# Batch 0 without expert pieces, batch 1 in units of 256, constant matmuls in waits, and expert 1's weights issued later

## The chip, the cores and the metric

The kernel runs on one core of one Trainium2 chip. The metric is the device time of one execution in microseconds (us); lower is better. TensorE (PE in the profile) does the matmuls, VectorE (DVE) and ScalarE (ACT) read their results out of PSUM, GpSimd (POOL) casts and issues the transfers that convert weights to 16 bits, and SyncE (SP) issues all other transfers. PEld is TensorE's loading of the stationary operand.

## What is computed

Attention with a sliding window of 128 and a linear bias over 8 batches of 576 positions with 8 heads of 64, and behind it a layer of 8 experts over all 4608 tokens, each token's experts weighted by a table P that comes out of 8 rounds of row and column normalisation:

```python
scores = scale * np.matmul(q, k.transpose(0, 1, 3, 2))
scores = np.where(mask, scores + bias[None], -1000000000.0)
attn = np.exp(scores - np.max(scores, axis=-1, keepdims=True))
x = (attn / attn.sum(-1, keepdims=True)) @ v      # then [4608, 512]
P = np.exp(x @ w_gate - max)
for _ in range(8):
    P /= P.sum(1, keepdims=True) + 1e-09
    P /= P.sum(0, keepdims=True) + 1e-09
    P *= N / E
for e in range(E):
    out += P[:, e:e + 1] * (np.maximum(x @ w1[e], 0.0) @ w2[e])
```

## The kernel before

**Two parts.** The first 340 us hold the attention of the 8 batches and, woven into it, experts 0 and 1, which do not need P: their results go to a scratch tensor and are weighted later. The rest of the time belongs to the normalisation and to experts 2 to 7 over 18 groups of tokens. The change is in the first part only.

**The order is written out by hand.** The kernel says in which order instructions stand; each engine takes its own in exactly that order, and waits at the first that isn't ready. Nothing overtakes. The same holds for the two queues of transfers: SyncE's (q1 in the profile) and GpSimd's (q0).

**A batch.** Its q and k come in as 1 MB each (`load_qk`, L232), v in five blocks of 128 positions (`load_v`, L334; the last has 64), the last 64 rows of q and k as a "tail" (`load_tail`, L223). `cast_qk(b, j)` (L247 for k on ScalarE, L245 for q on VectorE) converts a quarter of the heads to 16 bits. For batches 0 to 2 TensorE turns them (`turn_pe`, L311, eight 128-wide transposes for the k and q of one quarter), and ScalarE (L326) and VectorE (L324) copy the result out of PSUM. From batch 3 on DMA transposes do it. `cast_v` on GpSimd (L344) converts v.

**A step** is one block of 128 keys and one half of the heads: ten steps in a batch, written here (batch, block, half) or as step 0 to 9. `scores` (L372, L379) is four or eight matmuls, `exps` (L390) one exponential on ScalarE, `masks` (L403) one product with a table on VectorE (window and bias in one; `make_mask`, L209, makes the table on ScalarE with eight exponentials), `values` (L426) the product with v, of which a column of ones gives the denominator; VectorE takes the reciprocal (L436) and multiplies (L437). After both halves `turn_x` (L457) transposes the block and a copy (L465) puts it into xT, the experts' input. In the order of the code the next step's scores and exponential stand ahead of this step's values.

**The filler.** A unit is (expert, first block, number of blocks). Its layer 1 is 8 pieces (L102: 4 matmuls each, 128 columns for each block, then a ReLU on ScalarE, L109), its layer 2 one piece for each block (L115: 8 matmuls of 512 columns, then a copy by VectorE, L495 or L499). `Filler.take` hands out one piece; `fill(us)` hands out pieces until their planned cost (0.87 us for a layer-1 piece of 4 blocks, half of it for 2, 1.74 for a layer-2 piece) is used up. A unit can start when its blocks are in xT (`ready`) and its expert's weights are allowed (`allowed`). A step's `budget` spreads what is ready over the steps that are left.

**Weights.** `load_weights(e)` (L86, L88) issues w1 and w2 of an expert on GpSimd's queue, 1 MB each as stored. Expert 1's are issued after step 1 of batch 0, allowed from step 4 of batch 1.

**Buffers.** Four PSUM buffers ("pmm") go round among transposes, values, layer 1 and layer 2; two more hold scores. Staging buffers for v and the tails: five; SyncE issues a load once the buffer's last reader is done.

## Time and profile before

| | us |
|---|---|
| median of 3 runs | 1060.77 (1059.07 to 1062.29) |
| the profiled execution | 1060.31 |
| its span | 1058.5 |
| TensorE busy | 1031.1 (97%), 9006 matmuls |
| VectorE, ScalarE, GpSimd busy | 631.7, 434.5, 77.4 |
| TensorE busy in 0 to 10, 10 to 20, 20 to 30 | 3.44, 8.07, 6.15 |
| TensorE busy in 50 to 60, 60 to 70, 70 to 80 | 6.70, 9.40, 10.00 |
| mean granted clock of TensorE | 0.998 |

The profile comes from one execution. Its page has the span in 40 slices of 26.5 us, with the busy tenths of each engine, the granted clock of TensorE in tenths, and the busy share of the 16 DMA engines. The views of the trace give the same by stretches of chosen length; a list in order of time gives the start, the length, the engine, the line, the operation and, in brackets, how long the engine sat idle before it and what released it. A line of the waits is: who waited for whom, us in total, times, longest. A line of the chain is: start, length, what. A line of a DMA queue is: packets, MB, share of the 16 engines. [...]

### The profile page before, as it was taken

How to read it: one execution, taken by the hardware profiler on the slowest of the kernel's cores; microseconds unless marked ns; L12 is line 12 of the kernel's file. 1: busy time of each engine (PE TensorE's matmuls, PEld its weight loads, DVE VectorE, ACT ScalarE, POOL GpSimd, SP SyncE). 2: the span in 40 equal slices, each digit the busy share in tenths (PEclk: the TensorE clock that was granted, in tenths of full speed). 3: DMA queues.
4: the chain of work that ended last, by engine and by line, in shares of the span. 5: the costliest groups of instructions: out<-in, count | busy, mean ns of one | idle time of the engine just before them, and what ended most of it. 6: DMA issues, size and time to landing. Idle time of an engine off the chain costs nothing.

```text
span 1058.5 us, 21148 instructions
## 1 busy us (share of the span) xinstructions
PE 1031.1 (97%) x9006; PEld 802.9 (76%) x9006; DVE 631.7 (60%) x1171; ACT 434.5 (41%) x729; POOL 77.4 (7%) x139
## 2 busy tenths in 40 slices
PE   6789999999999999999999999999999999999998
PEld 4455444444544888888888888888888888888887
DVE  4655665655687665655655655655655655555555
ACT  6556555555233333333333333333333333333332
POOL 2112032325100000000000000000000000000000
PEclk9999999999999999999999999999999999999999
DMA  9985599879992501211211210211220220220240
GB/s 226 252 221 139 114 201 218 196 154 177 182 207 70 115 23 49 71 26 46 71 39 33 70 49 23 71 39 32 71 65 7 71 68 3 71 71 1 71 90 20
DMA packets 166110, 98.55 MB, mean 93 GB/s; under 512 B 84960, under 2 KB 157440, under 8 KB 166016
## 3 DMA queue, kind: packets, MB, share of 16 engines
q1 hardware_dynamic: 151280, 79.21, 29.4%
q0 software_dynamic: 14304, 17.84, 10.2%
q8 instruction: 70, 1.15, 0.4%
q14 instruction: 24, 0.20, 0.1%
q10 hardware_dynamic: 432, 0.16, 0.1%
HBM read 87.74 MB, written 19.02 MB: 101 GB/s over the span
## 4 chain that ended last, share of the span: by engine, by line
PE 92%; DMA 4%; SPq 2%; DVE 1%; ACT 1%; issue 0%; POOL 0%; ACTq 0%
PE psh L834 36%; PE psS_m L889 31%; PE psh L102 11%; PE psy L115 10%; DMA v<-in_v_dram 2%; DMA k<-in_k_dram 2%; PE psN L426 1%; PE psS L372 1%; DMA xT<-xsb 1%; SPq L334 1%; SPq L223 0%; SPq L288 0%; PE psy L954 0%; PE psG L473 0%; ACT hT L109 0%
## 5 line engine op out<-in xcount | busy, mean ns | idle before, releaser
L841 ACT ACTIVATE hs<-psh 128x512 f16<-128x512 f32 x432 | 258.0, 597 | 453.2 <-PE psh L834 373.7
L834 PE MATMUL psh<-aux,w1l 128*128 128x256 f16 x2880 | 372.6, 273 | 0.2 <-ACT hs L841 0.2
L834 PEld LDWEIGHTS <-w1l 128*128 128x128 f16 x2880 | 281.7, 98 | 33.3 <-issue 0.5
L889 PEld LDWEIGHTS <-hs 128*128 128x128 f16 x2568 | 251.3, 98 | 29.1
L846 DVE TENSOR_TENSOR hs<-hs 128x1024 f16<-128x1024 f16 x107 | 74.1, 693 | 274.5 <-ACT hs L841 274.3
L889 PE MATMUL psS_m<-w2l,hs 128*128 128x256 f16 x1440 | 186.6, 273 | 0.0
L102 PE MATMUL psh<-xT,w1t 128*128 128x512 f16 (+1 forms) x640 | 141.1, 359 | 4.4 <-DMA xT<-xsb 1.7
L115 PE MATMUL psy<-w2t,hT 128*128 128x512 f16 x576 | 133.8, 379 | 3.4 <-DMA w2t<-in_moe_w_dram 2.8
L818 DVE TENSOR_TENSOR aux<-xT,pbc 128x1024 f16<-128x1024 f16 x108 | 131.4, 1217 | 2.5 <-DMA pbc<-ptd 2.5
L109 ACT ACTIVATE hT<-psh 128x512 f16<-128x512 f32 (+1 forms) x160 | 87.6, 556 | 100.6 <-PE psh L102 99.3
L115 PEld LDWEIGHTS <-hT 128*128 128x128 f16 x576 | 53.7, 98 | 64.6 <-issue 4.8
L102 PEld LDWEIGHTS <-w1t 128*128 128x128 f16 x640 | 57.9, 99 | 53.6 <-issue 6.4
L390 ACT ACTIVATE pt<-psS 128x1024 f16<-128x1024 f32 (+2 forms) x80 | 67.5, 852 | 45.9 <-PE psS L372 37.0
L935 DVE TENSOR_TENSOR acc<-acc,psS_m 128x256 f32<-128x256 f32 (+1 forms) x162 | 74.3, 504 | 12.4 <-PE psS_m L889 11.1
L499 DVE CAST yo<-psy 128x512 f16<-128x512 f32 x68 | 46.9, 690 | 55.5 <-PE psy L115 54.3
L403 DVE TENSOR_TENSOR pt<-pt,mask 128x1024 f16<-128x1024 f16 (+2 forms) x80 | 50.2, 627 | 41.5 <-ACT pt L390 41.4
L889 PE MATMUL psS_m<-more,hs 128*128 128x256 f16 x576 | 74.6, 273 | 0.0
L834 PE MATMUL psh<-aux,w1t 128*128 128x256 f16 x576 | 74.6, 273 | 0.0
L849 DVE TENSOR_TENSOR hs<-hs 128x1024 f16<-128x1024 f16 x107 | 73.2, 684 | 0.0
L834 PEld LDWEIGHTS <-w1t 128*128 128x128 f16 x576 | 56.4, 98 | 6.5
L535 POOL DMA_DIRECT2D w2t<-in_moe_w_dram x2 | 1.8, 878 | 705.2 <-PE psS_m L889 669.8
L426 PEld LDWEIGHTS <-pt 128*128 128x128 f16 (+2 forms) x576 | 28.6, 101 | 26.1 <-DVE pt L403 6.8
(83 smaller groups left out, 657.2 us busy)
## 6 DMA issues: line engine op xcount, KB each, us to landing
pbc<-ptd SPq DMA_DIRECT2D x108, 128.0 KB, 4.5
y<-ysp SPq DMA_DIRECT2D x36, 256.0 KB, 4.7
ysp<-yo SPq DMA_DIRECT2D x68, 128.0 KB, 3.1
v<-in_v_dram SPq DMA_DIRECT2D x32, 256.0 KB, 3.9
out_dram<-acc SPq DMA_DIRECT2D x31, 256.0 KB, 2.4
q<-in_q_dram SPq DMA_DIRECT2D x7, 1024.0 KB, 6.4
k<-in_k_dram SPq DMA_DIRECT2D x7, 1024.0 KB, 9.8
w2t<-in_moe_w_dram POOLq DMA_DIRECT2D x4, 1024.0 KB, 14.7
```

What stands on the lines that cost most here:

```text
L102: nc.tensor.matmul(out=ps[:, 0:nt], lhsT=w1ts[e][:, dt, P * ft : P * ft + P], rhs=xT[:, b0 : b0 + nb, dt, :], start=(dt == 0), stop=(dt == ...
L109: nc.scalar.activation(out=st["hT"][:, ft, 0:nt], in_=ps[:, 0:nt], func=AF.Relu)
L115: nc.tensor.matmul(out=ps, lhsT=st["hT"][:, ft, P * ms : P * ms + P], rhs=w2ts[e][:, ft, :], start=(ft == 0), stop=(ft == NFT - 1),)
L390: nc.scalar.activation(out=pt[0:nk, :, 0 : nk + nn], in_=ps[0:nk, :, :, 0 : nk + nn].rearrange("p a y n -> p (a y) n"), func=AF.Exp, scale ...
L403: nc.vector.tensor_tensor(out=pt[0:nk, :, 0:w], in0=pt[0:nk, :, 0:w], in1=mask[0:nk, hs, 0:w], op=ALU.mult)
L818: nc.vector.tensor_tensor(out=xs(n).rearrange("p (d b t) -> p d b t", d=NDT, b=2), in0=xT[:, 2 * g : 2 * g + 2].rearrange("p b d t -> p d ...
L834: nc.tensor.matmul(out=ps[:, f, :], lhsT=W1L[e][:, dt, P * ft : P * ft + P], rhs=xs(n)[:, HB * dt : HB * dt + HB], start=(dt == 0), stop=( ...
L841: nc.scalar.activation(out=h[n][:, 2 * i : 2 * i + 2, :], in_=ps, func=AF.Relu)
L846: nc.vector.tensor_tensor(out=t[:, NFT : NFT + NF2, :], in0=a[:, 0:NF2, :], in1=a[:, NF2:NFT, :], op=ALU.add)
L849: nc.vector.tensor_tensor(out=t[:, NFT + NF2 : 2 * NFT, :].rearrange("p f n -> p (f n)").rearrange("p (f t) -> p f t", t=P), in0=a[:, :, P ...
L889: nc.tensor.matmul(out=Ms[g, bank][:, half, :], lhsT=left(n, m, f), rhs=W2L[e][RIGHT[m]][:, f, :], start=(e == 2 and f == 0 and half == 0) ...
L935: nc.vector.tensor_tensor(out=a, in0=a, in1=p2, op=op)
```

## The change

It makes these edits, all in the first part:

- Batch 0 takes no filler pieces, but for two layer-1 pieces in each of steps 6 and 7. At the end of batch 0 all layer-1 pieces of its four blocks that are left (12 of 16) stand in one stretch, then two layer-2 pieces, then batch 1's first transposes (`hold`, `budget`, the loop with `filler.take()`). Layer 2 is held back until there.
- The blocks 4 to 7 (batch 1) form two units of two blocks each for both experts, in place of one unit of four: 64 more matmuls, each half as wide.
- `spin` adds matmuls of 256 columns on a constant tile (the tile of ones, read as 16-bit numbers), whose results nobody reads: 20 at the start, 4 before and after batch 0's first scores and before its second transposes, 8 after the long layer-1 stretch, and 3 ahead of the value matmuls of each step of batch 0 and of steps 0 to 5 of batch 1: 88 in all.
- The second half of the mask table is made in two parts between the first casts; the first mask product stands behind the transposes.
- In batch 0 ScalarE copies x into xT, in place of VectorE.
- Expert 1's weights are issued after step 7 of batch 0 (on GpSimd's queue behind three more casts of v), and its units are allowed after step 8 of batch 1.
- Batch 2's casts and transposes move from steps 3 to 7 of batch 1 to steps 5 to 8. The load of batch 3's q and k stays at step 3 of batch 1, and its first cast at the end of step 8.

The order of SyncE's queue stays the same up to batch 2's last block of v.

```diff
     ident = per.tile([P, P], FP16, name="ident")
     ident32 = per.tile([P, P], FP32, name="ident32")
     ones32 = per.tile([P, P], FP32, name="ones32")
+    junk = ones32.bitcast(FP16)
     wg_sb = per.tile([P, NDT, E], FP16, name="wg_sb")
     rs_sb = per.tile([P, NBLK], FP32, name="rs_sb")
     cs_sb = per.tile([P, E], FP32, name="cs_sb")
...
             self.since = 0
             self.ready = 0
             self.allowed = {0}
+            self.hold = True
 
         def start_unit(self):
             for n, (e, b0, nb, make) in enumerate(self.todo):
...
             if not self.l1 and len(self.l2) <= 2:
                 if self.start_unit():
                     self.since = 0
-            use_l2 = bool(self.l2) and (not self.l1 or self.since >= 2)
+            use_l2 = bool(self.l2) and not self.hold and (not self.l1 or self.since >= 2)
             if use_l2:
                 self.l2.pop(0)()
                 self.since = 0
...
         mask = asb.tile([P, H, 2 * P], FP16, name="mask")
         rel = per.tile([P, HD], FP16, name="rel", tag="yo", bufs=YO)[:, 0 : 2 * P]
 
-        def make_mask(u):
-            for y in range(4 * u, 4 * u + 4):
+        def make_mask(ys):
+            for y in ys:
                 nc.scalar.activation(
                     out=mask[:, y, :], in_=rel, func=AF.Exp, scale=-float(slopes[head_of[y]])
                 )
...
         KT: dict = {}
         QKT: dict = {}
         vs: dict = {}
+
+        def spin(ps, n):
+
+            for _ in range(n):
+                nc.tensor.matmul(out=ps[:, 0 : 2 * P], lhsT=junk[:, 0:P], rhs=junk, start=True, stop=True)
+
+        spins = [0]
+
+        def spin_alone(n):
+            spins[0] += 1
+            spin(aps.tile([P, GT], FP32, name=f"psJ_{spins[0]}", tag="pmm", bufs=4), n)
 
         def load_tail(b):
             t32 = asb.tile([P, H, Dh], FP32, name=f"t32_{b}", tag="s32", bufs=5)
...
             if u == 0:
                 xsbs[b, kb] = asb.tile([P, H, Dh], FP16, name=f"xsb_{b}_{kb}", tag="xsb", bufs=3)
             psN = aps.tile([P, GT], FP32, name=f"psN_{b}_{kb}_{u}", tag="pmm", bufs=4)
+            if b == 0 or (b == 1 and 2 * kb + u < 6):
+                spin(psN, 3)
             psN = psN[:, 0 : 4 * Dh + 4].rearrange("p (h d) -> p h d", h=4)
             ops = []
             for y in range(2):
...
                         start=(j == 0),
                         stop=(j == NDT - 1),
                     )
-                nc.vector.tensor_copy(out=to, in_=ps[:, :, 0:nk])
+                if b == 0:
+                    nc.scalar.copy(out=to, in_=ps[:, :, 0:nk])
+                else:
+                    nc.vector.tensor_copy(out=to, in_=ps[:, :, 0:nk])
             else:
                 nc.sync.dma_start(out=to, in_=xsb[0:nk].rearrange("p h d -> p (h d)"), transpose=True)
 
...
             nc.vector.tensor_copy(out=yo, in_=ps)
             stores.append((e, blk, yo))
 
-        spans = [(0, 2), (2, 2)] + [(4 * g, 4) for g in range(1, NG)]
+        spans = [(2 * g, 2) for g in range(4)] + [(4 * g, 4) for g in range(2, NG)]
         order = [(0, 0), (0, 1)]
         for n in range(2, len(spans)):
             order += [(0, n), (1, n - 2)]
...
         nc.scalar.dma_start(out=rel, in_=rel_h.ap())
         nc.scalar.dma_start(out=ident, in_=ident_h.ap())
         nc.scalar.dma_start(out=ident32, in_=ident32_h.ap())
+        nc.vector.memset(ones32, 1.0)
         load_first()
-        nc.vector.memset(ones32, 1.0)
-        make_mask(0)
+        spin_alone(20)
+        make_mask(range(4))
         cast_v(0)
         load_weights(0, 0, 1)
         cast_v(1)
...
         steps = [(b, kb, u) for b in range(B) for kb in range(NKB) for u in range(2)]
         for j in range(2):
             cast_qk(0, j)
+            make_mask((4 + 2 * j, 5 + 2 * j))
+            if j:
+                spin_alone(4)
             turn_pe(0, 1, j)
             turn_pe(0, 0, j)
         cast_qk(0, 2)
         cast_qk(0, 3)
+        spin_alone(4)
         scores(*steps[0])
         exps(*steps[0])
+        spin_alone(4)
         turn_pe(0, 1, 2)
         turn_pe(0, 0, 2)
-        masks(*steps[0])
         turn_pe(0, 1, 3)
         turn_pe(0, 0, 3)
-        make_mask(1)
+        masks(*steps[0])
         for n, (b, kb, u) in enumerate(steps):
             nxt = steps[n + 1] if n + 1 < len(steps) else None
             at = 2 * kb + u
             left = ((8 if b < XPE else 10) - at) % 10 + 1
             budget = filler.backlog() / (11 if (b, at) == (XPE, 0) else left)
+            if b == 0:
+                budget = 1.0 if at in (6, 7) else 0.0
             if nxt:
                 if nxt[0] < XPE and nxt[1:] == (RI - 2, 1):
                     turn_pe(nxt[0], 0, NDT)
                 if nxt == (1, 0, 0):
+                    filler.ready = RI
+                    while filler.l1 or filler.todo[0][1] < RI:
+                        filler.take()
+                    filler.hold = False
+                    spin_alone(8)
+                    filler.fill(3.6)
                     cast_qk(1, 0)
                     cast_qk(1, 1)
                     for j in range(NDT):
...
                     scores(*nxt)
                     scores(*nxt[:2], 1)
                 exps(*nxt)
-            got = filler.fill(1.0)
+            got = filler.fill(1.0) if b else 0.0
             if nxt:
                 masks(*nxt)
             values(b, kb, u)
...
                     gates(4 * b - 4, 4 * b)
                 if n // 2 + NKB + 1 < B * NKB:
                     load_v(n // 2 + NKB + 1)
-            if b == 0 and at == 1:
+            if b == 0 and at == 7:
                 load_weights(1)
+            if (b, at) == (1, 8):
+                filler.allowed.add(1)
             if b == 1 and at == 4:
-                filler.allowed.add(1)
                 nc.sync.dma_start(out=ysp[0, 0:RI].rearrange("m p d -> p m d"), in_=first_y[0])
             if (b, at) == (0, 3):
                 load_qk(2)
...
                 homes(1)
             if (b, at) == (1, 3):
                 homes(2)
-            if b == 1 and 3 <= at <= 6:
-                cast_qk(2, at - 3)
-            if b == 1 and 4 <= at <= 7:
-                turn_pe(2, 1, at - 4)
-                turn_pe(2, 0, at - 4)
+            if b == 1 and 5 <= at <= 8:
+                for j in ((), (0, 1), (2,), (3,))[at - 5]:
+                    turn_pe(2, 1, j)
+                    turn_pe(2, 0, j)
+                for j in ((0, 1), (2,), (3,), ())[at - 5]:
+                    cast_qk(2, j)
             if 1 <= b < B - 2 and at == 3:
                 load_qk(b + 2)
             if 1 <= b < B - 2 and at >= 8:
```

## The prediction

> **What bounds the kernel now.** I read the page's slices first, then the chain of work that ended last for 35 to 75 us, then the waits up to 70 us, and last the DMA queues in stretches of 2 us.

> ```profile
> PE   6789999999999999999999999999999999999998
> PEclk9999999999999999999999999999999999999999
> DMA  9985599879992501211211210211220220220240
> ```

> TensorE is short of work only in the first three slices (79 us), and there the DMA engines are full. From 66 us to the end TensorE loses about 7 us in all. So the change can win only what the start loses, and the start is fed by DMA.

> ```profile
> 37.10 17.45 DMA k<-in_k_dram
> 54.55 0.03 ACTq L247
> ...
> 54.62 0.62 ACT c L247
> 55.23 0.49 ACT tT L320
> ...
> 57.96 1.55 PE psh L102 x8
> ...
> 66.71 0.87 PE psh L102 x8
> ...
> 72.54 1.73 PE psy L115 x8
> ```

> Batch 2's k takes 17.45 us to land. ScalarE's cast of it stands in the middle of batch 1 (L247, in program order), so ScalarE and then TensorE stop:

> ```profile
> ACT c L247 <- DMA k<-in_k_dram: 5.8, 3, 2.9
> PE psX L457 <- ACT tT L320: 2.9, 1, 2.9
> ```

> After that gap the granted clock is half, and eight 256-wide matmuls take 1.55 us where they take 0.87 at 66.71:

> ```profile
> 56.00:58.00 2.00, 2.00 (x29) 1.66 (x27) 1.29 (x4) 1.95 (x4) 0.00 (x0) 0.50 1.25 223
> ```

> Why does k take so long? Expert 1's weights are issued at 38.28 and share the engines. In 40 to 42 us SyncE's queue (q1) is alone; in 46 to 48 and in 52 to 54 it runs beside w1 and w2 on GpSimd's queue (q0):

> ```profile
> q1 hardware_dynamic: 620, 0.62, 96.8%
> ```

> ```profile
> q0 software_dynamic: 147, 0.30, 79.0%
> q1 hardware_dynamic: 152, 0.16, 28.0%
> ```

> ```profile
> q0 software_dynamic: 302, 0.31, 90.6%
> q1 hardware_dynamic: 302, 0.10, 31.4%
> ```

> Both queues get the same number of packets, and the weights' packets are 2 KB (w1) and 1 KB (w2). So q and k fall from 310 packets per us to 76, then to 150. The two loads (512 and 1,024 packets) last 15 us, from first bytes at about 43.4 (49 packets in 42 to 44) to the landing of w2 at 58.9 (issued 39.01, 19.9 on the way), and let through only some 1,540 packets of SyncE's queue.

> **The change, by its parts.** I count the TensorE work that each kernel has behind it at one time, and price it warm: a layer-1 piece of two blocks 0.43 (half of 0.87), a layer-2 piece 1.73, eight transposes 0.45, a value group 0.24, a score group 0.27, an xT transpose 0.22.

> *Up to 35.2 us.* The order of SyncE's and GpSimd's transfers is unchanged here, so their landings stay: v of the last block 23.7 (cast at 23.80), expert 0's w2 at 30.3, batch 1's k at 35.1. Batch 0 without expert pieces gets through its steps earlier, then waits for that v. The twelve remaining layer-1 pieces follow from 24.9 to 30.1 (12 x 0.43), the eight constant matmuls take 0.9, two layer-2 pieces end at 34.5. Then it waits for k, as before:

> ```profile
> 35.17 1.14 ACT L247 CAST c<-k 128x512 f16<-128x512 f32 x2 [2.33 <-DMA k<-in_k_dram]
> ```

> So nothing that speeds up batch 0 ends earlier; it only fits in 8 more layer-1 pieces (3.5 us). The split mask gives back about 0.8 us (ScalarE's second four at 11.87 to 13.2 held the exponentials), the five xT copies cost ScalarE 0.59 for VectorE's 0.41 each; both vanish in the wait for v.

> *Constant matmuls.* 88 of 256 columns: 0.11 us warm, 0.19 at half clock. The first 20 take 3.9 us and end before the first cast at 5.30. Behind those in batches 0 and 1 the value matmuls are queued, which wait for VectorE's mask anyway; at worst the last six are in the open, 0.7 us, and the wait below swallows that.

> *35 to 63 us.* Batch 1 starts about 0.8 us earlier (scores at 41.2, not 41.99), since two layer-2 pieces stand between its transposes instead of eight layer-1 pieces. Steps 0 to 4 have no filler and run at the pace of mask, reciprocal, product and xT copy (0.68, 0.17, 0.42, 0.41 and waits): about 2 us a step, to 52. From there 8 layer-1 pieces, 2 layer-2 pieces, batch 2's transposes and the rest of the attention are 11 us: TensorE is at step 8's end at about 63; before it was there at 73. Batch 2's k is no longer late: without the weights q and k of batch 2 (2,048 packets) need 6.6 us from 38.7, and land near 46.

> *The wait that takes its place.* At the end of step 8 ScalarE casts batch 3's k. Queued behind it are the exponential of (2,0,0) and every ReLU of expert 1's first unit; TensorE can issue three more layer-1 pieces and stops for a PSUM buffer. Before, that cast waited for nothing:

> ```profile
> 73.16 0.61 ACT L247 CAST c<-k 128x512 f16<-128x512 f32 x1
> ```

> because k had landed at 71.2 (issued 61.23, 10.0 on the way). When does it land now? The weights move on GpSimd's queue behind the casts of v(1,1), v(1,2) and v(1,3). The last lands at 47.5 to 48, the issue follows at about 49, first bytes 2 to 5 us later (row: 38.28 to 43.4): 52.5. Until then SyncE's queue moves v(1,4) and batch 2's first three v (1.3 us each: 1,024 packets, of which 1,575 passed in 10 to 12 us). Then batch 3's q and k stand beside the weights: 1,540 of 2,048 packets pass by 67.6, the other 508 take 1.6: 69.2. From the other side: the same bytes ended at 71.2, with the engines 0.62 busy from 58 to 62, 1.5 us of slack: 69.7. I take 69.7, and keep 67.5 and 72.5 as ends. Cast, exponential and ReLU follow (0.62, 0.92, 0.41): TensorE goes on at 71.7.

> *Sum.* Done by then, against before at 72.54 (layer-2 piece of the chain above): five layer-1 pieces fewer (-2.16), two score groups, two value groups and one xT transpose more (+1.24), six layer-2 pieces in both. That is before's state at 72.54 - 0.92 = 71.6. So 0.1 us is lost, and 1.85 for a second start at half clock: in 55.77 to 59.51 (3.74 us) the old kernel did work worth 1.89. Before had paid this as well, inside its 71.6. Expert 1's w1 lands about 60, w2 about 68, both before their use. The two issues on GpSimd's queue (0.74 and 0.89) now stand ahead of its cast of v(1,4), which is due near 51 and used near 60: nothing. What is left is the same work in another order. The units of 256 cost TensorE nothing (eight 256-wide 0.87, four 512-wide 0.86), ScalarE 3.6 us (32 x 0.41 against 16 x 0.60), which is free half the time. Later gaps (0.5 at 113, 0.7 at 137, 2.0 at 150 to 154 us) may move by 1.5 either way; I take none. Total +1.9: 1060.31 (span 1058.5 and 1.8 around it) becomes 1062.2. The median lies 0.46 above that execution: **1062.7**.

> [...]

> **Rivals.** *Batch 3's k is there in time.* Were SyncE's queue not slowed by the weights, q and k would land at 52 + 6.6, near 60, and TensorE would pass the marker at 65.5: -6.1, 1054.7. It decides at 63.5 us; each us later costs one. For it: weights that start late, or a share above 76 packets per us. Against it: the equal packet counts. *Batch 3's k comes still later, and the change is slower.* DMA engines are uneven: batch 2's q and k had nearly all their bytes over by 51, and landed at 54.55, 3.5 later. Such a tail puts k at 72.7 and the sum at +4.9: 1065.7. It is slower than can be told apart (0.3%, 3.2 us, is about what a measurement of this kernel separates from no change) once k lands after 71. Against it: q and k of batch 1 had a tail of 2 only. *Batch 0 itself ends sooner* is no rival, since k of batch 1 has nothing in its way that moved.

> **How the numbers follow.** Forecast 0.50: -2 to +5 us by its bounds (k 67.5 to 72.5, half clock 0 to 1.9, later gaps 1.5), that is 1058.8 to 1065.8 alone; of it faster 0.04, same 0.30, slower 0.16. k in time 0.25, faster. k later 0.25: slower 0.23, same 0.02. Faster 0.29, same 0.32, slower 0.39. The range 1054.5 to 1066.5 leaves out the outer part of each rival.

> **What would show it.** Right: ScalarE's cast of batch 1's k still at 35.2; batch 2's k no longer waited for; a wait of ScalarE's cast for batch 3's k of 5 us or more that ends near 70, TensorE idle beside it, and a granted clock near 0.5 behind it. Wrong: that cast not waiting, packets of SyncE's queue above those of GpSimd's while the weights move, or the later gaps changed by more than 2 us.

## The result, and the profile after

The changed kernel takes **1062.63 us** (median of 8 runs, 1061.06 to 1064.53), the kernel before 1060.25 beside it: ratio **1.0025, 95% interval 1.0015 to 1.0036**. It is slower by 2.4 us: less than the 0.3% below which the prediction calls two kernels the same, though the interval leaves out 1. The profiled execution took 1061.06 (span 1059.3), 0.75 more than the one of before. Run once more, beside the last experiments, it took 1064.23, ratio 1.0040 (1.0026 to 1.0054).

The slices of the page, as shown for before:

```profile
PE   8889999999999999999999999999999999999998
PEclk9999999999999999999999999999999999999999
DMA  9996399869992501201201211211220220220240
```

TensorE's first three digits were 6, 7, 8 and are 8, 8, 8: it is busier up to 53 us, in part with constant matmuls, and no time was won.

ScalarE's casts of k in order of time (start, length, what, idle before): batch 1's at 35.04, batch 2's in the next three lines without a wait, and batch 3's at 69.85.

```profile
35.04 1.14 ACT L260 CAST c<-k 128x512 f16<-128x512 f32 x2 [3.24 <-DMA k<-in_k_dram]
...
58.11 1.13 ACT L260 CAST c<-k 128x512 f16<-128x512 f32 x2
62.57 0.64 ACT L260 CAST c<-k 128x512 f16<-128x512 f32 x1
65.28 0.62 ACT L260 CAST c<-k 128x512 f16<-128x512 f32 x1
69.85 0.62 ACT L260 CAST c<-k 128x512 f16<-128x512 f32 x1 [1.23 <-DMA k<-in_k_dram]
```

So the wait for batch 2's k is gone, and one for batch 3's has come, where the prediction put it (69.7), but only 1.23 us long. TensorE in the same view:

```profile
53.88 1.13 PE L103 MATMUL psh<-xT,w1t 128*128 128x256 f16 x8 [1.64 <-DVE xT L483]
...
60.27 1.03 PE L103 MATMUL psh<-xT,w1t 128*128 128x256 f16 x8 [0.93 <-ACT hT L110]
...
69.40 0.29 PE L385 MATMUL psS<-qN,kN 64*128 64x256 f16 x2 [0.75 <-DVE qN L337]
...
71.09 3.97 PE L103 MATMUL psh<-xT,w1t 128*128 128x256 f16 x32
```

It does not stop for batch 3's k here (nothing in brackets at 71.09). It stops at 52.2 to 53.9, in batch 1, for VectorE's xT copy, which stands behind a mask, a reciprocal and a product on that engine. Behind that gap the granted clock is down (stretch, length, TensorE busy, its weight loads, VectorE, ScalarE, GpSimd, clock, DMA share, GB/s):

```profile
52.00:56.00 4.00, 2.36 (x28) 1.99 (x26) 2.25 (x5) 1.44 (x3) 0.43 (x2) 0.84 1.07 215
56.00:60.00 4.00, 3.34 (x30) 2.54 (x28) 1.30 (x5) 2.56 (x6) 0.66 (x2) 0.74 1.13 239
```

It is 0.50 in each us from 55 to 58. A mean of 0.84 and 0.74 over 4 us each is then 1.28 + 2.08 = 3.4 us at half clock, 1.7 us lost. TensorE's waits between 40 and 170 us (who for whom, us in total, times, longest), their three largest lines:

```profile
PE psy L116 <- ACT hT L110: 2.3, 3, 1.0
PE psN L441 <- DVE pt L416: 2.1, 4, 0.8
PE psh L103 <- DVE xT L483: 1.6, 1, 1.6
```

The first line was, before:

```profile
PE psy L115 <- ACT hT L109: 0.6, 1, 0.6
```

A unit of two blocks gives TensorE half as long a cover in each PSUM buffer (0.43 us of layer 1, not 0.86) while ScalarE is busy with a cast and an exponential (0.61 at 74.50, 1.03 at 75.01), and the first layer-2 piece behind it (76.36, 85.55, 95.76) waits for the ReLU.

### The profile page after: what moved, and what is told of

It is laid out like the page before. It is cut to its first block, busy times and chain, and to the rows that moved or that the text cites. A ratio compares the mean times of both kernels' runs of the same rounds, so it can differ in the third digit from the quotient of the medians.

```text
span 1059.3 us, 21466 instructions
## 1 busy us (share of the span) xinstructions
PE 1041.2 (98%) x9158; PEld 815.6 (77%) x9158; DVE 631.7 (60%) x1166; ACT 439.8 (42%) x750; POOL 78.5 (7%) x139
## 4 chain that ended last, share of the span: by engine, by line
PE 85%; DVE 0%; ACT 0%; issue 0%
PE psh L867 36%; PE psS_m L922 31%; PE psy L116 8%; PE psh L103 8%; PE psN L441 1%; PE psS L385 1%; PE psy L987 0%; PE psG L491 0%; DVE yo L517 0%; PE psX L472 0%; PE psC L792 0%; DVE pt L416 0%; ACT hs L874 0%; PE psP L807 0%; DVE L_sb L795 0%; PE psS L392 0%
## 5 line engine op out<-in xcount | busy, mean ns | idle before, releaser
L110 ACT ACTIVATE hT<-psh 128x512 f16<-128x512 f32 (+1 forms) x176 | 90.0, 521 | 107.2 <-PE psh L103 105.1
L116 PEld LDWEIGHTS <-hT 128*128 128x128 f16 x576 | 53.9, 98 | 63.6 <-issue 4.3
L103 PEld LDWEIGHTS <-w1t 128*128 128x128 f16 x704 | 64.8, 99 | 48.6 <-issue 6.1
L403 ACT ACTIVATE pt<-psS 128x1024 f16<-128x1024 f32 (+2 forms) x80 | 67.5, 851 | 28.2 <-PE psS L385 26.9
L416 DVE TENSOR_TENSOR pt<-pt,mask 128x1024 f16<-128x1024 f16 (+2 forms) x80 | 53.3, 667 | 41.1 <-ACT pt L403 40.9
L867 PEld LDWEIGHTS <-w1t 128*128 128x128 f16 x576 | 56.4, 98 | 6.5
```

The source lines that it names most:

```text
L103: nc.tensor.matmul(out=ps[:, 0:nt], lhsT=w1ts[e][:, dt, P * ft : P * ft + P], rhs=xT[:, b0 : b0 + nb, dt, :], start=(dt == 0), stop=(dt == ...
L110: nc.scalar.activation(out=st["hT"][:, ft, 0:nt], in_=ps[:, 0:nt], func=AF.Relu)
L116: nc.tensor.matmul(out=ps, lhsT=st["hT"][:, ft, P * ms : P * ms + P], rhs=w2ts[e][:, ft, :], start=(ft == 0), stop=(ft == NFT - 1),)
L403: nc.scalar.activation(out=pt[0:nk, :, 0 : nk + nn], in_=ps[0:nk, :, :, 0 : nk + nn].rearrange("p a y n -> p (a y) n"), func=AF.Exp, scale ...
L416: nc.vector.tensor_tensor(out=pt[0:nk, :, 0:w], in0=pt[0:nk, :, 0:w], in1=mask[0:nk, hs, 0:w], op=ALU.mult)
L867: nc.tensor.matmul(out=ps[:, f, :], lhsT=W1L[e][:, dt, P * ft : P * ft + P], rhs=xs(n)[:, HB * dt : HB * dt + HB], start=(dt == 0), stop=( ...
```

## The experiments

All ratios are to the kernel before, run beside each. "After again" is the changed kernel, run beside experiments 10 to 12. It was not run beside experiments 1 to 8: these can only be held against its two ratios, 1.0025 and 1.0040. The theories of the first four expectations come back under other letters later: S (then W) holds that landings beside expert 1's weights set the time, batch 3's k above all; P (then O) that the order and pace of the engines' own work does.

**1. No constant matmuls** (all calls of `spin` emit nothing).

> The changed kernel without its 88 constant matmuls. Theory S (the transfers pace the start, and TensorE has time to spare in it): all 88 lie in waits, so within 1 us of the changed kernel's 1062.6. Rival H (they hold the clock up in the thin steps of batch 1, 44 to 53 us): the clock halves some 5 us earlier, each half-clocked stretch costs about 1.9 us, so 1064 to 1067. Rival C (they stand in the way of the values): 1060 to 1061.5.

Measured 1062.41, ratio 1.0034 (1.0021 to 1.0047): no difference from after. Yet the clock did not stay up:

```profile
44.00:48.00 4.00, 2.05 (x31) 1.35 (x31) 3.11 (x9) 3.33 (x5) 0.00 (x0) 0.77 1.31 237
48.00:52.00 4.00, 3.84 (x48) 2.75 (x48) 3.68 (x6) 1.25 (x3) 3.77 (x9) 0.50 0.86 154
52.00:56.00 4.00, 2.75 (x32) 2.10 (x33) 2.83 (x9) 2.15 (x3) 0.72 (x2) 0.50 1.08 210
56.00:60.00 4.00, 4.00 (x28) 2.93 (x26) 1.28 (x4) 2.11 (x6) 0.66 (x2) 0.52 1.13 239
```

That is 13.7 us at half clock. It costs nothing, since TensorE only comes later to batch 3's k, which lands at 70.34 (ScalarE waited 0.51 for it). The constant matmuls do keep the clock up in batch 1 (with them it is 1.00 from 44 to 52 in after and after again, and 0.997 to 1.000 over the whole of their executions; in run 1 0.992 to 0.995), and nothing is bought with that.

**2. Batch 1 in units of 512 again.**

```diff
-spans = [(2 * g, 2) for g in range(4)] + [(4 * g, 4) for g in range(2, NG)]
+spans = [(0, 2), (2, 2)] + [(4 * g, 4) for g in range(1, NG)]
```

> The changed kernel with batch 1 in one unit of four blocks for each expert, as before. Theory S: the wait for batch 3's k ends at the same time (cast near 69.9), but steps 5 to 8 of batch 1 have nothing to fill in: 8 layer-1 and 2 layer-2 pieces (6.9 us) are missing at that point; the later waits of layer 2 for ScalarE (0.96, 0.84, 0.54 us) go. About +4.6, 1067. Rival P (small pieces are what costs): -2.3, 1060.3.

Measured 1069.18, ratio 1.0094 (1.0080 to 1.0108). ScalarE's cast of batch 3's k, and TensorE's first matmul behind it:

```profile
72.28 0.62 ACT L260 CAST c<-k 128x512 f16<-128x512 f32 x1 [10.54 <-DMA k<-in_k_dram]
```

```profile
74.36 1.86 PE L103 MATMUL psh<-xT,w1t 128*128 128x512 f16 x4 [8.46 <-ACT hT L110]
```

A unit of blocks 4 to 7 can't start before batch 1 is over, so TensorE has nothing to do until k is there. This is the wait of the prediction in full length.

**3 and 4. No load of expert 1's weights**, in after and in before (`load_weights(1)` hands back expert 0's tiles: expert 1 is computed with expert 0's weights).

> The changed kernel with expert 1 computed on expert 0's weights, so that expert 1's weights are never loaded (this part of the computation is changed). Batch 3's k should land near 60 and not 69.9. Theory S: TensorE is released from the input, 4 to 6 us less, 1057 to 1059. Rival P (the steps of batch 1 run at the pace of ScalarE, VectorE and the half clock, and arrive at that cast at 68.6 anyway): only the 1.2 us of the wait, 1061.4.

> The kernel before with the same edit: expert 1 on expert 0's weights, no second load. Theory S: batch 2's k lands near 46, the wait of 2.9 us and the half clock behind it (1.85) go: 4 to 5 us less, 1055 to 1056.5. Rival P: the wait goes and VectorE and ScalarE wait elsewhere in batch 1: less than 2 us.

Measured 1060.47, ratio 1.0017 (1.0003 to 1.0032), and 1058.20, ratio 0.9986 (0.9976 to 0.9996). With no weights on the way no cast of batch 2's or 3's k waits, and by the ratios still only 1 to 2.5 us go. (Five executions of run 3 had a granted clock of 1.000 and took 1058.3 to 1060.3, seven had a lower one and took 1060.2 to 1064.9, so its median depends on how often the clock fell.) In after without the load TensorE's waits of 40 to 100 us are the engines' own:

```profile
PE psy L119 <- ACT hT L113: 2.3, 3, 1.0
PE psh L106 <- DVE xT L486: 1.5, 1, 1.5
PE psh L106 <- ACT hT L113: 1.1, 1, 1.1
PE psS L388 <- DVE qN L340: 1.1, 2, 0.7
```

So the landings are not the whole cause. Run 4 fits P (less than 2 us), run 3 lies between the two theories.

**5, 6 and 7. The order in batch 1 and the cast.** Run 5 puts the value matmuls of step 5 ahead of the first piece of blocks 4 and 5; run 6 moves batch 3's casts one step later; run 7 does both.

```diff
-got = filler.fill(1.0) if b else 0.0
+got = filler.fill(1.0) if b and (b, at) != (1, 5) else 0.0
...
-if 1 <= b < B - 2 and at >= 8:
+if b == 1 and at == 9:
+    cast_qk(3, 0)
+if b == 2 and at == 0:
+    cast_qk(3, 1)
+if 2 <= b < B - 2 and at >= 8:
     cast_qk(b + 2, at - 8)
```

> In the profile of after TensorE stops for 1.64 us at 52.2 to 53.9: the first layer-1 piece of blocks 4 and 5 stands ahead of the value matmuls of step 5 of batch 1 and waits for VectorE's xT copy; the clock is half behind it (54.8 to 58.8). Here the value matmuls stand first. Theory O (the order of the engines' work in batch 1 costs the time): the gap falls under 1 us, no half clock between 52 and 60, 1.9 to 2.5 us less than after, about 1060.4. Theory W (batch 3's k, delayed by expert 1's weights, sets the time): TensorE only reaches the cast of batch 3's k sooner, that wait grows from 1.2 to about 3 us and still ends at 69.9; 0 to 0.5 us less than after, about 1062.4.

> Batch 3's first casts stand one step later, behind the exponential that they held up. Theory W: the wait of 1.2 us for batch 3's k no longer holds the exponential and the ReLUs; 1 to 1.2 us less than after, about 1061.4. Theory O: the half clock and the order of the engines stay, and ScalarE's cast then stands ahead of the ReLUs of the first layer-2 pieces instead; 0 to 0.4 us less, about 1062.4.

> Both edits. Theory W: the wait for k is passed by a step of 2 us or so, so what the earlier values win (1.9 to 2.5) shows now, and 1.2 more: 3 us less than after, about 1059.6, and more than the sum of the two alone. Theory O: the sum of the two alone, about 1060.2.

Measured: 1063.85, ratio 1.0034 (1.0021 to 1.0046); 1061.82, ratio 1.0016 (1.0005 to 1.0027); 1060.85, ratio 1.0009 (0.9995 to 1.0023). Run 5 lost the half clock at 55 and won nothing:

```profile
72.98 0.62 ACT L260 CAST c<-k 128x512 f16<-128x512 f32 x1 [3.20 <-DMA k<-in_k_dram]
```

```profile
72.00:76.00 4.00, 2.01 (x21) 1.44 (x19) 1.42 (x4) 2.83 (x7) 0.13 (x1) 1.00 0.83 195
76.00:80.00 4.00, 4.00 (x27) 2.85 (x26) 0.11 (x1) 2.80 (x7) 1.95 (x6) 0.57 0.66 156
```

The wait for k was 3.20 us and not 1.23, TensorE stood still for 1.99, and the half clock came behind that gap instead (0.57 over 4 us is again 3.4 us). This is W's picture, but the edit is not shown to be its cause: this execution started 3.5 us later (scores of batch 1 at 45.75, in after 42.22), and the unchanged kernel waited 3.66 us in run 9. Run 7 gets past the cast, and its ratio is below that of either edit alone, though the intervals overlap. Against 1.0025 for after, the two edits together win more than their sum, as W says; against 1.0040 they win just the sum, as O says. So runs 5 to 7 do not decide between the two.

**8. The later weights alone, in the kernel before** (issued at step 7 of batch 0, allowed at step 8 of batch 1, as in the diff).

> The kernel before with one part of the change alone: expert 1's weights issued at step 7 of batch 0 (not 1), its pieces allowed at step 8 of batch 1 (not 4). Theory W: the wait for batch 2's k (2.9 us) and its half clock (1.9) go, and batch 3's k, which the weights now delay to about 70, takes their place at the cast at the end of step 8; TensorE goes on near 71.7 as in both kernels: within 1 us of before. Theory O: batch 3's k costs about 1.2 us, and the rest is won: 3 to 4 us less than before, about 1056.5.

Measured 1067.17, ratio 1.0065 (1.0051 to 1.0080). Both theories were wrong on the size: the wait for batch 3's k is far longer than the one for batch 2's that it replaces.

```profile
70.38 0.62 ACT L247 CAST c<-k 128x512 f16<-128x512 f32 x1 [8.54 <-DMA k<-in_k_dram]
```

**9. After again**, as it is.

> The changed kernel itself, run beside the others of this call. Its profile shows whether the half clock in batch 1 and the landing of batch 1's k and q are the same in another execution. Theory W (batch 3's k lands 21 to 22 us behind the issue of expert 1's weights and sets the marker at about 72): 1.0025 to before, within 0.0015. Theory J (the start moves from one execution to the next by as much as the change does: scores of batch 1 began between 41.99 and 45.75 in the profiles so far): the scores begin anywhere from 42 to 46, and the span moves with them.

Measured 1064.23, ratio 1.0040 (1.0026 to 1.0054). Its scores of batch 1 began at 42.42, those of run 12 beside it at 45.31, so the start does move as J says; the span does not move with it (run 12 starts later and is shorter). This execution had no half clock at 52 to 60, though TensorE's gap there was the same (1.61 us). ScalarE reached the cast sooner and waited longer, though not the 5 us of the prediction; TensorE's stop and the half clock behind it came as predicted:

```profile
71.03 0.62 ACT L260 CAST c<-k 128x512 f16<-128x512 f32 x1 [3.66 <-DMA k<-in_k_dram]
```

```profile
72.89 4.68 PE L103 MATMUL psh<-xT,w1t 128*128 128x256 f16 x28 [2.45 <-ACT hT L110]
```

```profile
68.00:72.00 4.00, 2.29 (x22) 1.60 (x22) 0.42 (x2) 0.97 (x2) 0.00 (x0) 1.00 1.06 320
72.00:76.00 4.00, 3.11 (x16) 2.17 (x16) 1.53 (x4) 2.51 (x7) 0.73 (x3) 0.57 0.94 201
```

**10. Expert 1's units four blocks wide.**

```diff
-order = [(0, 0), (0, 1)]
-for n in range(2, len(spans)):
-    order += [(0, n), (1, n - 2)]
-order += [(1, len(spans) - 2), (1, len(spans) - 1)]
+order = [(0, s) for s in spans[0:4]] + [(1, (0, 4))]
+for g in range(2, NG):
+    order += [(0, (4 * g, 4)), (1, (4 * g - 4, 4))]
+order += [(1, (4 * NG - 4, 4))]
...
```

> After with expert 1's units four blocks wide from the first; expert 0's stay two wide up to block 7. If the units of 256 cost TensorE the waits of its layer-2 matmuls for ScalarE's ReLU (0.96, 0.84 and 0.54 us at 76, 86 and 96), these fall to under 0.6 in all and the time by 1 to 2 us against after. If those waits only stand in for another (ScalarE's casts and exponentials come at the same places), the time stays within 0.5 us of after.

Measured 1061.14, ratio 1.0014 (0.9999 to 1.0030), against 1064.23 of after beside it: 3.1 us less. The line of 2.3 us is now

```profile
PE psy L116 <- ACT hT L110: 0.2, 1, 0.2
```

while the wait for batch 3's k was as long as ever (4.05 us, to 71.22).

**11. Expert 1's weights early again, in after** (issued at step 1 of batch 0).

> After with expert 1's weights issued at step 1 of batch 0 again, as before; its pieces are still allowed at step 8 of batch 1. Theory W: batch 2's k is late again (about 54.6) and batch 3's is not waited for; with units of 256 and no pieces of expert 1 TensorE stands still for some 3 to 5 us in batch 1: 2 to 4 us slower than after, about 1065.5. Theory O (the order of the engines' work costs more than the landings): within 1 us of after.

Measured 1063.15, ratio 1.0033 (1.0020 to 1.0047): the same as after beside it. W was wrong here. Batch 3's k is not waited for; instead batch 1's v of block 3, which stands behind batch 2's q and k on SyncE's queue, is late:

```profile
59.71 0.55 PE L441 MATMUL psN<-v,pt 128*128 128x65 f16 x7 [3.08 <-POOL v L358]
```

Behind that gap the clock is half for 3.4 us again (0.87 and 0.71 over 4 us each from 56 on). Early or late, the weights share the engines with something that is due within 20 us: issued at 38.42 here, with v due at 56.63; issued at 48.96 in after, with k due at 68.62.

**12. All of 5, 6 and 10, and the weights behind batch 3's q and k.**

```diff
-if b == 0 and at == 7:
+if b == 1 and at == 5:
     load_weights(1)
```

> After with the values ahead of the first piece at step 5, batch 3's first casts one step later, expert 1's units four wide, and expert 1's weights issued at step 5 of batch 1, behind batch 3's q and k. Theory W: q and k have the engines to themselves and land by 58 instead of 70, so neither the casts nor the half clock remain; 2 us less than after as without the load at all, 1.2 more for the layer-2 waits: about 1059, within 0.2% of before or faster. Rival: the weights now come late, w1 after 71 or w2 after 76, and expert 1's first pieces wait for them: each us late costs one, and the time is 1063 or more.

Measured **1057.64**, ratio 0.9985 (0.9969 to 1.0001): 6.6 us less than after beside it, and 2.2 less than before. The interval still reaches 1, so that it beats before is not shown. GpSimd issues the weights at

```profile
56.94 0.74 POOL L87 DMA_DIRECT2D w1t<-in_moe_w_dram  x1
```

and TensorE waits for no weights and no k: the lines of its waits from 40 to 170 us that come to 0.9 us or more are

```profile
PE psh L103 <- ACT hT L110: 1.6, 2, 1.1
PE psN L441 <- DVE pt L416: 1.1, 2, 0.9
PE psS L385 <- DVE qN L337: 1.1, 2, 0.7
PE psh L103 <- DMA xT<-xsb: 0.9, 1, 0.9
PE psT L324 <- DVE c L258: 0.9, 1, 0.9
```

The rival (weights too late for expert 1's first pieces) did not come. Between the profiles of after again and of this run, TensorE's idle time from 36 to 170 us falls from 13.1 to 6.8 us, and 1.7 us of half clock go: 8.0 us. The later start (45.31 against 42.42) gives back 2.9 of it, and the two profiled executions differ by 4.8.

What the new place of the weights adds to the other three edits is not shown. From after again's 1.0040, run 10 takes off 0.0026 and run 7 0.0031; that alone would make 0.9983.

## Why the prediction came out, point by point

The total was right (1062.7 against 1062.63; as a difference to before, +1.9 against +2.4), and a wait for batch 3's k does take the place of the one for batch 2's. But two terms in between were wrong, and that the total fits is in part luck: the wait was shorter than forecast without ending at another time, and the cost of the narrow units was met by other gaps that happened to shrink.

- **Up to 35.2, same landings: right** in the profiled execution (k's cast at 35.04, not 35.17). The 3.5 us of layer 1 fitted in: 64 of its matmuls stand before 36 us, in before 32. But TensorE did not wait for v at the end of batch 0: the twelve pieces began at 25.97, not 24.9, the two layer-2 pieces ended at 35.7, not 34.5, and TensorE waited 0 (after again 0.46) us for k. The 0.8 us that batch 1 should start earlier did not show (scores at 42.22, before 41.99).
- **Constant matmuls free: right** (run 1), though the first 20 took 4.45 us, not 3.9.
- **Batch 2's k no longer late: right.** No cast of it waits in after.
- **Batch 3's k at 69.7: right**, 69.85 and 71.03. While the two queues share the engines they still move equally many packets, here in 60 to 62 us of after:

```profile
q0 software_dynamic: 240, 0.25, 72.0%
q1 hardware_dynamic: 241, 0.25, 44.4%
```

  In all runs in which ScalarE waited for this k with the weights issued at 48.7 to 51.3 us, it came 20.9 to 21.7 us behind that issue (after 48.96 to 69.85, run 2 51.06 to 72.28, run 8 48.68 to 70.38).
- **"TensorE is at step 8's end at about 63": wrong, this is the step that failed.** ScalarE was free for the cast at 68.62 in after and 67.37 in after again. The count of 11 us of work from 52 took TensorE as busy throughout. In after again it stood still for 3.54 us between 52 and 68, for VectorE's xT copy (1.61), ScalarE's ReLU (1.14) and smaller ones; in after for 2.66, with 1.7 of half clock besides. About 1 us more in each stays open. So the wait for k was 1.2 to 3.7 us, not more than 5. It still ended when k came, which is why the total did not show the error.
- **Half clock behind the k wait, 1.85: right in size and kind, not always in place.** 1.7 us, behind the k wait in after again and runs 5 and 10; in the profiled execution of after it came at 55, and no second one followed. In all four, and in run 11, the clock was at half for 3.4 us (a mean of 0.57 over 4 us in after again and run 5, of 0.79 over 8 us in run 10). The gaps of TensorE ahead of it were 1.64 us in after, 1.99 in run 5, 2.45 in after again, 2.83 in run 10 and 3.08 in run 11.
- **"The units of 256 cost TensorE nothing": wrong.** I compared the pace of the matmuls (eight of 256 columns 0.87 us, four of 512 0.86) and left out what each unit gives as cover: 2.3 us of waits for ReLU, 3.1 us of time in run 10. Luck hid it in the total: TensorE's idle time from 72 to 160 us is 3.98 before, and 4.45 after with the 2.3 inside, so the other gaps shrank by 1.8. One wait of before for xT, 1.70 us at 152.93, is not there in after. (ScalarE's extra 3.6 us is 3.5 by the prediction's own figures.)
- **Sum.** For after again: 0.1 as predicted, TensorE going on at 72.89 and not at 71.7 (1.2), half clock 1.7, and 0.8 more idle time from there to 160 (4.81; before 3.98 from 72) make 3.8; measured 1064.23 - 1060.31 = 3.9. For the profiled execution of after, the fastest of its eight, the same sum gives 0.0 (TensorE going on at 71.09, the half clock already in that, 0.5 more idle time); measured 0.75, and the rest stays open.
- **The rival "k in time" needed 63.5 us**; without the load at all (run 3) k came in time, and that gained 1 to 2.5 us, not 6.1, for the same reason: TensorE is not there at 63 (ScalarE reached the cast at 67.14).

Each part, then: constant matmuls 0; later weights alone +6.9 (run 8); with units of 256 they cost no more than the early ones (run 11); these units save 6 to 7 against 512 (run 2) and cost about 3 where expert 1 uses them (run 10), of which 2.1 is seen in waits. What batch 0 in one stretch does by itself was not run.

## What to carry to other kernels

A load that is moved out of the way of one transfer can delay the one that then runs beside it (a wait of 8.54 us for k in run 8, of 3.08 for v in run 11): before moving it, list what is due in the 20 us after its new place (here k landed 20.9 to 21.7 us behind the weights' issue). Issuing it behind that is worth trying; run 12 does so, together with three other edits, and is the shortest of all that compute the whole. Where a landing comes last, what the work ahead of it costs can stay hidden: 13.7 us at half clock ahead of k changed nothing (run 1). That speeding such work up only lengthens the wait, so that two edits together win more than each alone, is likely but not shown here (runs 5 to 7). Smaller pieces are not free at equal pace, since each gives the engine that reads its result less time (0.43 us a piece and not 0.86: TensorE's largest line of waits for ScalarE's ReLU is 2.3 us in after and 0.2 in run 10).

## What the runs showed of the hardware

```profile
26.00 0.60 POOL L357 CAST v<-v 64x512 f16<-64x512 f32 x1 [2.76 <-DMA v<-in_v_dram]
```

  so that batch 1's scores began at 42.42 and 45.31, though the instructions stand in the same order up to there. The profiles of runs 5, 6 and 7 started late as well (44.9 to 46.0), and no other later than 43.72. All four have an edit of run 5 or 6, which come only later in the program; with one profile each this may be chance. Why v lands later in these stays open. For this reason the medians, not the single profiles, carry the comparisons above.
